# Reversing the score matmuls of the third query block in a fused state read and gated causal attention, with a new table of the order of steps

## The chip, the cores and the metric

The kernel runs on one core of one Trainium2 chip. The core has a matrix engine (TensorE, in the rows PE, with its weight loads as PEld), VectorE (DVE), ScalarE (ACT), GpSimd (POOL) and SyncE (SP). Each works through its own list of instructions in order, and semaphores make one engine wait for another. Here SP issues all DMA transfers, those that transpose among them. The metric is the device time of one execution in microseconds (us). The profiled execution of the kernel before took 310.0 us; its trace covers a span of 308.2 us of it.

## The reference

`x` is 8 batches x 8 heads x 512 rows x 64, `state` is 8 x 8 x 32 x 64. The reference has two stages:

```
a     = softmax(x @ state^T / 8);  xread = a  @ state     (512 rows read 32 slots)
a2    = softmax(state @ x^T / 8);  sread = a2 @ x         (32 slots read 512 rows)
y     = concat(xread, sread), heads side by side          (8, 544, 512)
logits = y @ w_gate;  w = softmax of the two largest of 4 (top 2 of 4 experts)
out   = sum over the two experts e of  w_e * (softmax(causal(q_e @ k_e^T / 8)) @ v_e) @ wo[e]
        with q_e = y @ wq[e], k_e = y @ wk[e], v_e = y @ wv[e], head width 64
```

`wq` and `wk` are drawn 200 times larger than the other weights, so the scores of the experts are large and need about fp32 accuracy.

## The kernel before, in words

Every fp32 operand of a large product is split into a high and a low f16 part, and a product is three f16 matmuls (high x high, high x low, low x high, `PROD`). The splits, the softmax and the evictions from PSUM are shared by ACT, DVE and POOL. Matrices that a product needs transposed (`xT`, `a2t`, `qm`, `pt`, `z`) are made by SP's transposing DMAs from their untransposed f16 form (`xh`, `a2`, `qh`, `ph`, `zh`).

A batch goes through these functions: `load` (its `xn` tiles of 512 KB and the state `sn`), `front` (scores against the state, their block transposes `eb` and maxima `mb` on DVE, the softmax `at`, the state's products with the weights `gs`, then `kt`, `qf` to `qh` to `qm`, and `v` as products of `at` and `gs`), `state_scores` and `side` (the slots that read the rows: `m`, `e`, `a2`, `a2t`), `probs` (causal scores of query blocks of 128 rows), `reads` (the probabilities times `v`, then times `wo`, then the store of `o`) and `tail` (the 32 state rows of two batches at once). `probs(b, unit)` is called for the units (0, 1), (2,) and (3,), which are the blocks of 128 query rows of a batch.

In `probs` (the lines around 811 to 866) the scores of the experts go to two PSUM banks `sp[0]` and `sp[1]`. A bank belongs to one of the two chosen experts of a row; three of the four experts can be that one, and the queries of those not chosen are zero. One step of PE does all of it: first matmuls that use all 128 rows of the array (two of the three experts at once), then the causal mask, added by a matmul with an identity, and then matmuls with 64 rows (the third expert), in pairs for the two banks that stand side by side in the upper and the lower half of the array. Then DVE takes the maxima (`mx`), ACT the exponentials (`p`), ACT and POOL or DVE split them into `ph`, and SP transposes `ph` to `pt` for `reads`.

The order of the work is not that of the code. The functions only record steps, 1959 in all. A step has an engine or a choice of engines (`either`: for example a multiplication of 192 columns on DVE or three of 64 columns on ACT). The function `run`, line 257, replays them by three packed tables in `ORDER`, line 22: the order of all steps, the engine that was chosen for each, and the buffer that each tile takes. All instructions are issued in `run`, so nearly every row of the trace has line 265 and tells its step only by its operand names. The buffer of a tile sets what it must wait for: the earlier readers of the same buffer, and with eight PSUM banks (`bank`) that is the most common wait of PE. On SP a transfer's issue also waits where the rings that it uses are still occupied.

Of the kernel before, what the change touches and what calls it, by code (L numbers as in the profile page):

```python
# [14 lines left out]
AF = mybir.ActivationFunctionType  # L15
# [8 lines left out]
        "c-jrtV`C5s6adico0pAc+peu;+qP|cwQSqAZQHhOzxVn4fs+CNQbKA#NCgDRfuR8iG=}=n6ch}afI~QF1eu^Agog-_9U?*`$PAGo2NZ-TkOy"
        "*OA;<zbAu9wxUWf|0Ar0ikT#ym+K_N;D>7g(bgM63=(?JkqgA5Q11)vC&fM!q*N<w}p3Z<Y7l!X@19O^;^$d45v8dQUh5FP4345$t<p$fEwS"
        "Wp^bLsh5;ai9~lf?f~;#i29Qgw{|V;zA{e2elwRw1L`?0NO$gNC;h^9rT4h&=tBtcSr>Npgr`59#8;#!zJhd1+g#=fSynY4?+<P!l7^(4nYV"
        "O#p5stu0Sv@fZb3Wk3ccJ276%#T!mvW7($^kT!)iz14`ggH~|A;EZl@$FdA;bZP){6pd=25J1`2y!7x||iD43qfPHWn?m`j>gQ+kX7Qrc)1|"
        "wk#9DwOi3Kzo+*a>4`CM<!|Fa*xSEU1d(VLue6voIS<V?mk&=U^4wgSk)!=fQm_i)&y$T!3o00v^ChSc<FRB2>q<uo0F*4J<<Ipd2oPO|Ti("
        "!%AF+6QCvrLV4T*MQJ%agjKi!CPENxh1IwmgQ)`6!WCE%>tiw62F<V>Rl?fX3b#XJObQKf4YtPS*aR!%T1*BZR0o@48;ry)a2+<p;#8iVL0z"
        "nZ>#-%)!_riN8es`)i%;M=l%yBX2{&MSd<oy69lnAt7@0fcBZ$JK=rxp~H_!ne!&~T%PvJYfgR;~Ie?Uj<iCwV=Zp8P%*bn>SPl&*uVH5s>F"  # L30
        "Yp_N;AZ>^192!0!frSgKfoUl{0qY{B3C5E!Pp-SC*p8){0JkkDviW&Sc$e^6B>Y@U>t^GO&W!OlW;Un$1vQAV{j@W#^M?@4QC?Z3=H6Z5SyD"
        ")be@ORXck7oxI7;h;B1V_ad<q&;{cq1+i?yyqv{k7BTG~akF_W{Zo}rZ5ToH-+<}WQKE~k5*ny^CbgWJBIR-|c1h^RMPzp?lEoccw#$Ff`>r"
        "zT=NfB@-cBIbKiDF@8szO~T6?Ub1v<rLV8mdo`DI!LsM7SG!&{}Fht!NK+qjj_wThmG0hYcwTwW0kOlMmo}YD5PyF-E~tm>M@wV~UN3@H9rH"
        "!x%tmFcL-Mo)nGFU`A|9NAN6mr|5JH+fi&vf^jGY#lhp)p5oF*ib*H17saB?coffJJlaJ4C=<q~OPGKYP!{Y@2`Ld}#XwApiRnBhp@f_b`%o"
        "Zd;sG>`Hd9hc#z`?5CFkChh?7%dPQimHicF^zl!Q}qc1%gbXa=RCK)!$vF%2c<%={WJV=7KfSvVO!!k*lhw$Meqg2Sm75236)m{N0Zev6MWj"
        "M8BrPD^p|4aSlun2!4LR+>o(WDJE;Y>6ugWdvQtI5LYy(L0PT@nj^8rh$}=XH!HOOX)F@q^F_OkH=9Ad5YONzKo~-oP%@V1WLp2aU!MVNtBU"
        "3U<Mk%Uoj^>!%UQuGt*?sLf0@IKgR%>N8j-}=HdmEmD2Nex-L;=DP^NvG=*Zy4U8sp=o{X|<usLk;9MHW+36O}rwp8fa?>`tjrn*PW#k>Sf("
        "mm%zJoX91?J{E@(~Mhe$K-SDX|pbm$-=TVqVTkc_@hQN)cX3*<>*l<;EP$PbG=mlU0;e0;L$Il%$eMmQYE~E={-@CzD5#Lw;gvxi68VDVOCm"
        "GKib=YRXGM$z=$);CuKBQ^;VxkEQv66z5!+Q~F35et;GEx;~atjI@)UNo9T_M13Wfgm6D$D#2Aax11!QN?e}HaeqlGN)>p3<dI#JS3Y4n*-b"
        "V0p`@2RRFkh#2H8uWF{7NKeYBr`<7ukJ2WTh{luUAvu5(p38YGA43{~U9bW^JHF>1}%C<C6Q+T50p&~v#Z=cp6c;p=ps>hcZ#gSU9F)Z^Q7o"  # L40
        "a*xpYQQ(CA$Q?M+>%@IUpzra=>oN5r(4v9GfP)4C^xx1XOW8(j&Ac6?!fuv4i}QUTto`XJ^F_)B)=4u+tiUea{&pG4>Cl8<-K&{KXQkP$yE)"
        "Jm-3Kq=y18O#pN~qmaF`j-bi=8OU-12yroC<Rvz$B`73wy3AL10a*5u_1N|rWskwZVhgw43&_lk)!{jM_rBZT_Kgnf!#4V(iyu#OVpL=j?xk"
        "6>+89mZ(R9c4dQ!TEK`L2GJcT`U9X$gI%U!<&jr+hS=-%|y7!k{C#ygaA;R7FN|Nv$L$r2tiyDg2bH$qx$Us`6Y>KhP*1&5t#VfgjLR{zzYC"
        "3|EwAOj<)q=~y1e-{d)$)^_rOr}1|ot}Y#<wjjS`))(}O7ujo`&NbyHz2PT1o@a1ZdCN1I`5o7hAM%Udb9ec`;i-()m5Ka`g+I|pp1^bYr__"
        "?qTu)~47ycz*`6Y>drr$K1Rp;>nt}mwF_zN}=<?lR)8_ExEBtN;V{^G{cL?-bc`pr$HjV$DH+E)IsYkTP?J!B1|7*FP#+EKRgEnUZdsgvB+M"
        "I25S+gk1{i+KmX&?UT`BWpzct<HaWDU)=Oml|F_Xe3?6<+Z0o(0?3`m-Bo5qX&4cebnXlMk{C~&7x8Dldj;mI-mdQXYD1~HJV1zgPc_Z^bqI"
        "K750x-*?Jx+uPBEe<}bR=Ug=7Er<FCQZZMDy94fu#wN})XJWBrQXbF?zwp3YG+Zg#mW2J<Nl(ccO#<Kk%H<g_nUB}BR-pH%DlueLp8e3y3+A"
        "f|b@wK$YQnFJVSHJ3RKEjh^nQmf}gc?Iv=uwWNiFCOp)-$}(Cd+g=&HtkXY7#ADXE}j>)0Dc0<LOHMuA6y=tkQElMP|x*{-KL>3m@ZknoMVj"
        "%X*zH$#trfwS2lkH`yFXrAc*~gp<XZLR0GknJcR`ji%MDoKBb6JSnV8ZM}t;qMBYa=rY^O8Fh{R)J(ci=1XSHrMY#j{?f&=QS)n%ZqmG3&Nk"
        "~J*`h_XfNs@rwoUi(b}gt&Bv>QcQaR31Exaw09a>0>X*63dYU?G6MX;T+LN<z7L<_JG-E1pmr@BS5!?MM8%PQGzC-?&IvJG;~qT3!jDp@Ro9"  # L50
        "FbkJNsh^CiD}1eudR{IvfZj^Ry$!kY^&|GJ+ehkS~lA&*=?&Fm#VtWs_7}KuF?D=@8^Az!(vzs&1vQB5}&qxR#R)~ev56jb(hAn_;$eR=owq"
        "0yS0h#(deGgVt8FmWc4(r@71^#$F|8qtFN)Vp*Gchn!p-qGd-Y*t-0>kv(`Xc=s`UzhpeR@(m*?Bhi$u@<h9aPV|xc(Cyn*I?3WXg#8O%uKP"
        "M;UuwIakdQn<wC%q(bJ(+dZc-C6`Xcs-A!!$hi)1%r~4@fFYYW=m1rnat{+)~&89ii=XxaP5edQ1;WK1*Zm^|*G^w01~FYC0=yp_<+<%L&b3"
        "MJ=OcvYwjDPHJX5CAqD;p3?l5*D6>g8>fS`vK6o*7GwqOik#L$7HskSh)vL9c3LjkC=IcMeoo{2QLAWIC6QmZ1m4we*m=8bXY{I#*9%s~y7@"
        "J`Xt(T&jn<nsQGeNOo1|5(hhOGuHd)U|b!%e3t%mi`^V&;mT5qjoXSKF9wK~?!>e?S`Zhx(wwXpiu((c#=ZEFqeqCT+h-pU%<6T4@v?Vr7{M"
        "+W}PX6P$>YK`o!y|nw**xJ}bdv34oy}hw^#{SmY+bsQHGgW<ue6)A=$@<u5o2_4Ln9b3z*4O&kH~Vf8{D=KCbn-|(SH&Z`d4C(Mk==cOMez<"
        "c(57fO5AY#+O-5KxA8ujV(R%qvi|YNnzjv|$9%|#Pvpu#hHp+VYJniG1ysM43Zr0PrXn3Eh-7T?CuxZ-ECR$&gWRq>65Ayk%#0UFy?PWte(0"
        "kiZ9qQ?Pfe!PeKFEf9G9Te1J=8~ea=)abJ-v^%FrQ&#JcVcQ%i7t;dPX1TsePel@{~T_2ir{R;;DRsXZBe((P!Hb%kFb5i)ZyImdhvkWY6YP"
# [9 lines left out]
        "c-l=<36_O02qUcbzwv~i-|2g5Tec*i!6U23?hCh=t~5Tdn(+!V7+=G0wS5Z?bF(zWn0J{mg)B{H=i302&ju?*?z<~z_*&c7!COuVVBr4T0AW"
        "bl1AAyj(JR|9yrD0W?mQZrho~*Mi87oHLF{*qD>i&3!X1YvBYD5odV$?qlb5#spzbYS{xNUcd{zX{x)%QMEV;5q@oGsRW5Ea6D4f+;mD|P5D"
        "BcnpOOt7s`|cnTL+nMseR0X$MHfgku1Gn;=LAfW6zA2S3IfHmQ?infMPiE%cvBPvn^3lviDbu*B#|>IDO}G}Q8f34vA)&g%O*VP9%pJw&ZF@"  # L70
        "-m!X}cMK?4^$C1@)LpwAn?aahhFk#@@c<MnE?FDblO?`GiX!uucn^?a&v$y;WqNIBU<QApn09a4zdKDT|2m17(RilVUTkCg<O>?xZS4V}e7T"
        "<QU@pX~p=#!ER5}Z@KJ(oGNq}_H*+V$Mzy2O(x#8k_YNA73mK!qTYYJUW~{{(+fQU*="
# [979 lines left out]
```

## Time and profile before

| what | value |
|---|---|
| runs of the kernel before | 305.06, 307.17, 308.19 us (median 307.17) |
| profiled execution | 310.0 us |
| its span in the trace | 308.2 us |
| PE busy | 285.8 us (93%), 3323 matmul records |
| DVE, ACT, POOL busy | 260.0 (84%), 226.1 (73%), 151.9 (49%) us |
| DMA packets | 165260, of them 144096 under 512 B; 53.95 MB |
| mean granted clock of PE | 0.983 |

A granted clock of 1.00 is the higher of TensorE's two levels, 2.4 GHz; the lower one is 1.2 GHz. A row of an engine gives the start in us, the duration, the engine and line, what is written and read (`out<-in`), the shape, and how many such instructions follow one another; in brackets stands the idle time before them, and the engine or transfer whose end released them.

### The profile page before, as it was taken

The page shows a single profiled execution, that of the slowest core. Times are in us where ns is not written, and L with a number is a line of the kernel's source. Part 1 is how long each engine was busy: PE and PEld are TensorE (multiplying, and loading weights), DVE is VectorE, ACT ScalarE, POOL GpSimd, SP SyncE. Part 2 cuts the span into 40 slices and gives each one's busy share as a digit, 9 for nine tenths or more (in the row PEclk, how much of TensorE's full clock was granted, in tenths as well). Part 3 has the DMA queues.
Part 4 walks back from the last instruction along what each step waited for, and adds up shares of the span by engine and source line. Part 5 has one row for each costly group of instructions (what it writes and reads, how often), then busy time and mean ns, then how long its engine had stood idle before and what let it go on. Part 6 is the DMA issues. An engine that isn't in the chain of part 4 may idle for free.

```text
span 308.2 us, 8993 instructions
## 1 busy us (share of the span) xinstructions
PE 285.8 (93%) x3323; PEld 193.7 (63%) x3323; DVE 260.0 (84%) x745; ACT 226.1 (73%) x690; POOL 151.9 (49%) x222
## 2 busy tenths in 40 slices
...
GB/s 194 223 124 203 154 156 183 234 177 172 138 202 203 168 180 213 171 177 197 207 142 245 185 234 175 125 185 178 83 146 176 91 209 126 95 172 205 184 213 152
DMA packets 165260, 53.95 MB, mean 175 GB/s; under 512 B 144096, under 2 KB 160736, under 8 KB 165216
## 3 DMA queue, kind: packets, MB, share of 16 engines
q1 hardware_dynamic: 165216, 53.37, 89.2%
...
q14 instruction: 18, 0.15, 0.2%
...
## 4 chain that ended last, share of the span: by engine, by line
PE 46%; DVE 21%; DMA 14%; ACT 12%; issue 4%; POOL 3%; SPq 0%; DVEq 0%; ACTq 0%; POOLq 0%
PE bank L265 46%; DMA xn<-in_x_dram 4%; DMA qm<-qh 4%; DVE mx L265 3%; DMA a2t<-a 3%; ACT p L265 2%; ACT z L265 2%; DMA pt<-ph 2%; DVE xh L265 2%; DVE mb L265 2%; DMA z<-zh 1%; DVE eb L265 1%; DVE qf L265 1%; DVE sbm L265 1%; DVE z L265 1%
## 5 line engine op out<-in xcount | busy, mean ns | idle before, releaser
L265 PE MATMUL bank<-kt,qm 128*128 128x128 f16 (+7 forms) x384 | 48.4, 305 | 4.6 <-DMA qm<-qh 4.0
L265 PE MATMUL bank<-gs,at 128*128 128x260 f16 (+3 forms) x368 | 50.7, 284 | 1.1 <-DVE eb L265 0.7
L265 PE MATMUL bank<-wo_n,z 128*128 128x512 f16 (+1 forms) x198 | 46.5, 373 | 2.8 <-DMA z<-zh 2.3
L265 PE MATMUL bank<-v,pt 128*128 128x192 f16 x480 | 45.5, 251 | 2.7 <-DVE kt L265 1.5
L265 PEld LDWEIGHTS <-pt 128*128 128x128 f16 x480 | 41.0, 100 | 6.7 <-issue 4.0
L265 PEld LDWEIGHTS <-at 128*128 128x128 f16 x336 | 32.1, 98 | 8.5 <-issue 2.3
L265 ACT ACTIVATE p<-bank,mx 128x128 f32<-128x128 f32 (+3 forms) x64 | 33.3, 526 | 4.3 <-DVE mx L265 3.9
L265 PEld LDWEIGHTS <-qm 128*128 128x128 f16 (+1 forms) x384 | 23.5, 98 | 18.7 <-DMA qm<-qh 4.6
L265 DVE TENSOR_REDUCE mx<-bank 128x1 f32<-128x128 f32 (+3 forms) x64 | 28.8, 478 | 7.7 <-PE bank L265 7.3
L265 POOL TENSOR_TENSOR ph<-p,ph 128x768 f16<-128x768 f32 (+1 forms) x15 | 28.1, 1875 | 7.4 <-ACT ph L265 4.8
L265 PEld LDWEIGHTS <-z 128*128 128x128 f16 x198 | 18.1, 98 | 21.7 <-DMA z<-zh 3.8
L265 ACT ACTIVATE o<-bank 128x512 f32<-128x512 f32 x30 | 17.8, 596 | 11.9 <-PE bank L265 11.8
L265 ACT ACTIVATE z<-bank,c 128x64 f32<-128x64 f32 x87 | 20.4, 320 | 6.8 <-PE bank L265 6.1
L265 ACT ACTIVATE xh<-xn 128x512 f16<-128x512 f32 x32 | 19.1, 629 | 7.3 <-DMA xn<-in_x_dram 6.4
L265 PE MATMUL bank<-at,gs 128*128 128x512 f16 (+1 forms) x92 | 24.2, 399 | 0.3 <-DVE m L265 0.3
L265 DVE SCALAR_TENSOR_TENSOR xh<-xn,xh 128x512 f16<-128x512 f32 x27 | 19.5, 741 | 3.9 <-ACT xh L265 3.8
L265 POOL TENSOR_TENSOR qh<-qf,qh 128x768 f16<-128x768 f32 x11 | 18.4, 1680 | 5.0 <-ACT qh L265 4.9
L265 POOL TENSOR_TENSOR eb<-eb,sbm 128x512 f32<-128x512 f32 x11 | 12.4, 1130 | 13.4 <-DVE sbm L265 12.0
L265 POOL TENSOR_TENSOR z<-z 128x128 f32<-128x128 f32 x15 | 7.0, 468 | 21.7 <-DVE z L265 9.5
L265 ACT ACTIVATE ph<-p 128x768 f16<-128x768 f32 (+1 forms) x17 | 15.6, 918 | 2.1 <-DMA pt<-ph 2.1
L265 ACT ACTIVATE gs<-bank 128x512 f16<-128x512 f32 (+2 forms) x29 | 13.7, 496 | 4.7 <-PE bank L265 4.6
L265 PEld LDWEIGHTS <-xh 128*128 128x128 f16 x416 | 15.1, 101 | 2.1 <-issue 0.8
...
## 6 DMA issues: line engine op xcount, KB each, us to landing
...
z<-zh SPq DMA_TRANSPOSE x29, 2.8
xT<-xh SPq DMA_TRANSPOSE x28, 3.3
...
```

The costliest lines, as they stand in the source:

```text
L265: f(**{k: v.ap() if isinstance(v, View) else v for k, v in kw.items()})
```

## The change

For the unit (2,) alone, the third block of every batch, the step of `probs` is issued in reverse: the pairs of 64-row matmuls first (now with the flag that starts the bank), then the masks, and the 128-row matmuls last (now with the flag that ends it). In the pairs of all units the upper half's matmul now stands ahead of the lower half's. The sizes passed to the planner's record follow. The three tables of `ORDER` are new: another order of steps, another engine for some, other buffers. The code below is the whole of the first part; of the tables one line stands for all.

```
@@ ORDER @@
-        "c-jrtV`C5s6adico0pAc+peu;+qP|cwQSqAZQHhOzxVn4fs+CNQbKA#NCgDRfuR8iG=}=n6ch}afI~Q...
+        "c-jrtgJKX06adico0pAc+peu;+qP|cwQSqAZQHhOzjwakqyT`FkQxwD0YP$LXaE9@L7_evGy#XE5DpqaCI...
...
@@ probs @@
+        turned = unit == (2,)
+        wide, paired = [], []
         for m, (a, c) in enumerate(PROD):
             for i in unit:
                 for s in range(2):
-                    g.append((part[s, i], qm[:, i, a, 2 - 2 * s], kt_[:, c, 1 - s, :w_[i]], m == 0 and i == i0, False))
-        for i in unit:
-            for s in range(2):
-                g.append((sp[s][:, at_[i] + i * P:at_[i] + w_[i]], identb, consts["maskb"], False, False))
-        for m, (a, c) in enumerate(PROD):
-            for i in unit:
-                g.append((part[1, i], qm[lo_, i, a, 1], kt_[lo_, c, 1, :w_[i]], False, m == 2))
-                g.append((part[0, i], qm[hi_, i, a, 1], kt_[hi_, c, 0, :w_[i]], False, m == 2))
-        st.mm(g, *((6, w_[i], 128, 1) for i in unit), (2 * nb, P, 128, 1), *((6, w_[i], 64, 2) for i in unit))
+                    wide.append((part[s, i], qm[:, i, a, 2 - 2 * s], kt_[:, c, 1 - s, :w_[i]], not turned and m == 0 and i == i0, turned and m == 2))
+                paired.append((part[0, i], qm[hi_, i, a, 1], kt_[hi_, c, 0, :w_[i]], turned and m == 0, not turned and m == 2))
+                paired.append((part[1, i], qm[lo_, i, a, 1], kt_[lo_, c, 1, :w_[i]], turned and m == 0, not turned and m == 2))
+        masks = [(sp[s][:, at_[i] + i * P:at_[i] + w_[i]], identb, consts["maskb"], False, False) for i in unit for s in range(2)]
+        full = [*((6, w_[i], 128, 1) for i in unit), (2 * nb, P, 128, 1)]
+        half = [(6, w_[i], 64, 2) for i in unit]
+        if turned:
+            st.mm(paired + masks + wide, *half, *full[::-1])
+        else:
+            st.mm(wide + masks + paired, *full, *half)
```

The number of matmuls stays at 3251, and the steps that they belong to keep nearly the same order on PE: 264 of its 305 steps stand where they stood, the others move by a few places. On the other queues more moves, and 187 of the 1959 steps change their engine; DVE issues 716 instead of 742 steps, ACT 521 instead of 518, POOL 232 instead of 209. Changes between the array's shapes along PE's list (128 rows, 64 rows, 32 rows, fewer columns) are 115 before and 117 now.

Three places of the new order. The first is DVE's list where the state scores of batch 4 are transposed (`eb_115` from two banks, the second of them bank_85), while the maxima `m` and `mb` of the same scores are taken and the last `kt` of batch 3 leaves its bank (`kt_135`). Before:

```order
L265 TENSOR_REDUCE m_0_145<-bank_85 128x1
L265 STREAM_TRANSPOSE eb_115<-bank_82 128x256
L265 TENSOR_SCALAR m_0_145<-m_0_145 128x1 [waits DVE_49]
L265 STREAM_TRANSPOSE eb_115<-bank_85 128x256
L265 STREAM_TRANSPOSE eb_115<-bank_85 128x256 [waits Activation_49]
L265 TENSOR_REDUCE mb_116<-eb_115 128x16 [waits DVE_49]
L265 TENSOR_REDUCE m_0_145<-bank_82 128x1
L265 TENSOR_REDUCE mb_116<-eb_115 128x16 [waits DVE_49]
L265 SCALAR_TENSOR_TENSOR kt_135<-bank_83,kt_135 128x512 [waits Activation_49]
```

The same piece of DVE's list in the changed kernel:

```order
L266 TENSOR_REDUCE m_0_145<-bank_85 128x1
L266 SCALAR_TENSOR_TENSOR gs_121<-bank_86,gs_121 128x260 [waits Activation_49]
L266 SCALAR_TENSOR_TENSOR gs_121<-bank_79,gs_121 128x260 [waits Activation_49]
L266 TENSOR_REDUCE mb_116<-eb_115 128x16 [waits DVE_49]
L266 STREAM_TRANSPOSE eb_115<-bank_85 128x256 x2
L266 SCALAR_TENSOR_TENSOR kt_135<-bank_82,kt_135 128x512 [waits Activation_49]
L266 TENSOR_REDUCE m_0_145<-bank_83 128x1
L266 TENSOR_REDUCE mb_116<-eb_115 128x16 [waits DVE_49]
L266 SCALAR_TENSOR_TENSOR kt_135<-bank_80,kt_135 128x512 [waits Activation_49]
```

The two transposes of bank_85 now follow each other without a wait for ACT between them, and `kt_135` stands ahead of one `m` and one `mb` that it stood behind.

The second place is SP's list while batch 2 is read and batch 3's queries are transposed: `pt_0_168` and `pt_0_169` are probabilities of batch 2 (units (2,) and (3,)), `qm_134` from `qh_142` and `qh_143` the two halves of batch 3's queries, `xn_89` a load of batch 6. Before:

```order
L265 DMA_TRANSPOSE pt_0_155<-ph_153 128x12x128 [waits DMAHW3_49,DVE_49]
L265 DMA_TRANSPOSE pt_0_168<-ph_154 128x12x128 [waits DMAHW4_49,Pool_49]
L265 DMA out_dram<-o_181 128x512 [waits DMAHW5_49,Activation_49]
L265 DMA_TRANSPOSE qm_134<-qh_142 128x12x128 [waits DMAHW6_49,Pool_49]
L265 DMA sn_87<-in_state_dram 128x2x64 [waits DMAHW7_49]
L265 DMA xn_89<-in_x_dram 128x8x128 [waits DMAHW0_49]
L265 DMA_TRANSPOSE pt_0_169<-ph_153 128x16x128 [waits DMAHW1_49,Pool_49]
L265 DMA_TRANSPOSE xT_96<-xh_92 128x8x128 [waits DVE_49,DMAHW2_49,PE_49,Activation_49]
L265 DMA out_dram<-o_179 128x512 [waits DMAHW3_49]
L265 DMA_TRANSPOSE qm_134<-qh_143 128x12x128 [waits DMAHW4_49,Pool_49]
```

The same piece of SP's list in the changed kernel:

```order
L266 DMA_TRANSPOSE pt_0_155<-ph_153 128x12x128 [waits DMAHW2_49,DVE_49]
L266 DMA_TRANSPOSE xT_96<-xh_95 128x8x128 [waits DMAHW3_49]
L266 DMA out_dram<-o_181 128x512 [waits DMAHW4_49,Activation_49]
L266 DMA xn_89<-in_x_dram 128x8x128 [waits DMAHW5_49]
L266 DMA_TRANSPOSE qm_134<-qh_142 128x12x128 [waits DMAHW6_49,Pool_49]
L266 DMA_TRANSPOSE pt_0_168<-ph_154 128x12x128 [waits DMAHW7_49]
L266 DMA sn_87<-in_state_dram 128x2x64 [waits DMAHW0_49]
L266 DMA_TRANSPOSE pt_0_169<-ph_153 128x16x128 [waits DMAHW1_49,Pool_49]
L266 DMA_TRANSPOSE xT_96<-xh_92 128x8x128 [waits DMAHW2_49,DVE_49,Activation_49]
L266 DMA_TRANSPOSE qm_134<-qh_143 128x12x128 [waits DMAHW3_49,Pool_49]
```

The transpose of `pt_0_168` moves from ahead of the first `qm_134` to behind it and behind the load `xn_89`; the second `qm_134` no longer has a store of `o` ahead of it.

The third place is SP's list some 25 us earlier, where `qm_133` from `qh_142` and `qh_143` are batch 2's queries, `sn_87` a load of the state, `xT_96` from `xh_94` a transpose for batch 5 and `pt_0_169` probabilities of batch 1. Before:

```order
L265 DMA_TRANSPOSE pt_0_169<-ph_154 128x16x128 [waits DMAHW4_49,Pool_49]
L265 DMA_TRANSPOSE xT_96<-xh_94 128x8x128 [waits DMAHW0_49,DVE_49,DMAHW5_49,PE_49,Activation_49]
L265 DMA_TRANSPOSE qm_133<-qh_142 128x12x128 [waits DMAHW6_49,Pool_49]
L265 DMA sn_87<-in_state_dram 128x2x64 [waits DMAHW7_49]
L265 DMA_TRANSPOSE qm_133<-qh_143 128x12x128 [waits Pool_49]
```

The same piece of SP's list in the changed kernel:

```order
L266 DMA_TRANSPOSE pt_0_169<-ph_154 128x16x128 [waits DMAHW4_49,Pool_49]
L266 DMA sn_87<-in_state_dram 128x2x64 [waits DMAHW5_49]
L266 DMA_TRANSPOSE xT_96<-xh_94 128x8x128 [waits DMAHW0_49,DMAHW6_49,DVE_49,PE_49]
L266 DMA_TRANSPOSE qm_133<-qh_142 128x12x128 [waits DMAHW7_49,Pool_49]
L266 DMA_TRANSPOSE qm_133<-qh_143 128x12x128 [waits Pool_49]
```

The load `sn_87` moves from behind the first `qm_133` to two places ahead of it.

Elsewhere on SP the transpose to batch 2's fourth `z` moves ahead of one `pt` and one `a2t`. On PE the last product of `side` (`a2t,xh`, 48 matmuls, batch 7) moves ahead of the product of batch 4's fourth `z` with `wo`. On ACT, two of the conversions `xh<-xn` of batch 5 move ahead of the high half of the `kt_135` above, and the exponential `e` behind it. At the start ACT's high half of batch 0's last `kt` moves two places ahead, and on PE one more product moves ahead of its reader.

## Rows read from the trace of the kernel before

**Rows 1.** The page: busy time and share of each engine, and the DMA packets.

```profile
PE 285.8 (93%) x3323; PEld 193.7 (63%) x3323; DVE 260.0 (84%) x745; ACT 226.1 (73%) x690; POOL 151.9 (49%) x222
...
DMA packets 165260, 53.95 MB, mean 175 GB/s; under 512 B 144096, under 2 KB 160736, under 8 KB 165216
```

**Rows 2.** Chain that ended last: start, length, and what the time went to.

```profile
64.10 6.71 DMA qm<-qh
...
150.91 4.40 DMA qm<-qh
...
171.15 4.34 DMA z<-zh
...
245.91 59.10 PE bank L265 x565
```

**Rows 3.** Stretches: length, busy time (count) of PE, PEld, DVE, ACT, POOL, clock, DMA share, GB/s.

```profile
71.20:74.80 3.60, 3.60 (x51) 2.27 (x48) 1.27 (x6) 1.20 (x5) 1.72 (x5) 0.53 0.88 184
112.00:119.00 7.00, 4.73 (x32) 2.96 (x31) 4.30 (x11) 4.36 (x13) 3.73 (x4) 1.00 1.36 179
119.00:122.60 3.60, 3.60 (x25) 3.37 (x24) 3.60 (x10) 2.02 (x7) 1.65 (x4) 0.53 0.98 212
123.00:130.00 7.00, 7.00 (x62) 4.01 (x62) 5.10 (x16) 4.47 (x18) 3.83 (x6) 1.00 0.80 170
```

**Rows 4.** Timeline of PE: ends of a unit (2,) step, batches 2 and 4.

```profile
126.16 0.66 PE L265 MATMUL bank<-kt,qm 64*128 64x384 f16 x6
126.75 1.47 PE L265 MATMUL bank<-wo_n,z 128*128 128x512 f16 x6
...
194.31 0.66 PE L265 MATMUL bank<-kt,qm 64*128 64x384 f16 x6
194.81 0.28 PE L265 MATMUL bank<-tl,rep 64*128 64x4 f32 x2
```

**Rows 5.** Timeline of PE, 116 to 123 us.

```profile
116.40 0.82 PE L265 MATMUL bank<-gs,at 128*128 128x260 f16 x6 [0.74 <-DVE eb L265]
118.76 3.72 PE L265 MATMUL bank<-v,pt 128*128 128x192 f16 x24 [1.53 <-DVE kt L265]
```

**Rows 6.** Timeline of DVE, the same time.

```profile
115.90 0.45 DVE L265 STREAM_TRANSPOSE eb<-bank 128x256 f32<-128x256 f32 x1 [2.70 <-ACT e L265]
...
118.02 0.68 DVE L265 SCALAR_TENSOR_TENSOR kt<-bank,kt 128x512 f16<-128x512 f32 x1
```

**Rows 7.** Timeline of ACT, the same time.

```profile
114.57 0.63 ACT L265 ACTIVATE xh<-xn 128x512 f16<-128x512 f32 x1 [2.78 <-DMA xn<-in_x_dram]
```

**Rows 8.** Timeline of SP: start and length of an issue.

```profile
116.14 1.34 SPq L265 DMA_TRANSPOSE qm<-qh  x1
117.53 1.08 SPq L265 DMA_DIRECT2D sn<-in_state_dram  x1
...
140.55 1.47 SPq L265 DMA_TRANSPOSE qm<-qh  x1
...
144.33 4.44 SPq L265 DMA_TRANSPOSE pt<-ph  x1
...
150.23 0.58 SPq L265 DMA_DIRECT2D out_dram<-o  x1
```

**Rows 9.** Timeline of PE: other places at which it waits, and one read of `pt`.

```profile
36.29 0.38 PE L265 MATMUL bank<-kt,less 128*128 128x512 f16 x1 [2.16 <-ACT kt L265]
...
147.97 1.65 PE L265 MATMUL bank<-v,pt 128*128 128x192 f16 x18
...
155.36 1.15 PE L265 MATMUL bank<-kt,qm 128*128 128x384 f16 x6 [1.41 <-DMA qm<-qh]
...
175.53 1.47 PE L265 MATMUL bank<-wo_n,z 128*128 128x512 f16 x6 [1.65 <-DMA z<-zh]
...
222.14 0.97 PE L265 MATMUL bank<-kt,qm 128*128 128x384 f16 x5 [0.61 <-DVE v L265]
...
240.97 1.47 PE L265 MATMUL bank<-wo_n,z 128*128 128x512 f16 x6 [0.62 <-DMA z<-zh]
```

More of the change, by code (lines that the diff above doesn't have):

```diff
@@ L23 @@
     (
[L24 to L58, printed above, removed]
@@ L67 @@
-    (
[L68 to L72, printed above, removed]
+        "c-jrtgJKX06adico0pAc+peu;+qP|cwQSqAZQHhOzjwakqyT`FkQxwD0YP$LXaE9@L7_evGy#XE5DpqaCI}A=Ap&HF%n%WBKtad?ksuEgf}D"
@@ new lines @@
+        "^WvqD}-19>qU<br&d5AtAINDqaf0_4X+lpE4P4afkIAtRK70#FQ!LNh1>MIb+vg(wgLbszv*Kyhde6`>SVg%S`IT0%4^3DF@4szXPp3B8~dl"
+        "!o$92|7Uxs0T5j7PN+7hy|UY8pMV;&<EN;TxbjNpbNx@cF-5PLN}-j-Jw17gWAv^5<nH`0R^x(T!Icz5DVh~=m~}JAQZt<5QIbF5L|}iP!xk"
+        "P1VdprT!BGw60SmVEQVv@2wa1`umeWH0=N!Gp#<K5W3UTG!wI+v!(bc?hn;W>2EuJf2xnj_B!WE<1_fy$l*Bu*4+g_Dm;__sE-Zq>kQk=JWL"
+        "OL%-~g1uDKH*J!Vs7NOW-t|hqEvfO5-djO#7iK7NOZt2IoL!SOxcBE}Vn1I1kpqeOL-BU_MmC3$PL%z*1Zd7oj??g^f@S*TFJO0-IqItcR6Y"
+        "1B=o!2%;@80m|b;sENyA1FXV{uoYHg1q`O;SP@rXecT4cs2MiKK&XY=p%qrb=2#ocQ3H&`Nue?}!DJ9Zt#J)D#THlx*J2wiPV2BCmZxV>7pv"
@@ new lines @@
+        "fUEKT*W0=2{v)D|1zb0|rXxf5={C-4YfKzn=%-=GUVhF4IEqVQ`dL!I#rJcaJ~7QRC}EKBd81NOlm&=EIcPkawuk+CoSgdVsFBk(Wiho9j$Y"
+        "{r531%}{P_y9w35dML&7?FozHx&E}iWO-v_D93vI1xWWRdTFE<FFcyz%AH>CgDi@1T|>@hT<p;hocd2I))+Q7>vbJu?9`UnMfGG|6m5j=BBh"
+        "A=V4r)h0%FD&c_8<ouYCa4#3$MkK<u@Y({f1vMj{O7zrm}E!v9Fumd%x_&680;Ue6D$+0#?#l@Ha<8vK~!4YT*M#s7o11nPtT7n6&7pBCR*q"
+        "K_=PV7h#Fa<`WDij$zQ7o)SU1$v@!miYc>eE_Eg^_6&uA_+9fOcbR>WzD_8|}p&)P_!CL)wS?F*Qb^^%Rp2U?WP50dx>gVPo1rvGEX|#;DYt"
+        "4r3aOMA7INM!{%&1~Xz?icUxHEXJVN)RWp#9EyWUusy}4jTDoPV=szDneiN+z@r$CHc>yygz@P-Ucv;NfU;mhN<@7q5ED~>%8HvQ2_@ugn28"
@@ new lines @@
+        "f{AWfrWoD`!-Qc6b2IWecj<dlL3(EyrGDJTi2<digwGIJ`*j)6RbF5p8<%4z5|X5mzv3@_tg>P>xV2wlM~)RR+FTzrICxfiGA-h2_?U|M>M!"
+        "zmp;#xUx`v1AOr!vr#uo?u^&Epa6sZKV+uN>?$V%%V6lipJ7NiYL)!Hf7_X6j4S~ddklIIFSsb^f-=UNDh9A?{PfEm+jP_({K*VKojU0W~8q"
+        ";kv?Ef9>6&<EoY)@n2s}37P^k}C>KA+tdyPuWC3NP?>LFR;Zlk!lj#QLqU$n+ZsIoDLCYzoOr<##P3F=q%uWM21Lvk6IG=9g3d+biC?7AQLH"
+        "q*mU_s8!`T2$v;*YqHUSeVy%z1bb72v}B6Yoei$w_xHF9&fEzAG!~7v`a?a$g#A5?M@7C72^gQGO)%B)c@@Kv_jiIHe5XRFYJdP*X0(%{iIm"
+        "kdk~4Q%iCw%PFJ<r;*hJlvDCjA9*09xj2{N`&fn_U`2i=*A=O+?4-w%3(Ip_=_e&PmxOR7CVC?Mr81wS+%lAzDzH!$9w6m-7b)eD-Si35NnY"
```

39 lines of the change are left out of this document (34 added, 5 removed).

## The prediction

> **What bounds the kernel now.** I read the page first [rows 1]: PE is busy 285.8 of 308.2 us, DVE 260.0. The reader sees that PE leads, but that its idle time, some 22 us, is made by others. The chain of waits [rows 2] says where: from 245.91 us to the end it is one piece of 59.10 us of PE, without a wait, so nothing after 246 us can be gained unless PE gets less to do. Before it the chain leaves PE at several places, most often for a transposing DMA that took 4.34 to 6.71 us. The table of stretches [rows 3] gives the second loss: from 71.2 to 74.8 and from 119.0 to 122.6 us the granted clock is 0.53, close to the lower level of 1.2 GHz, and before the second of them PE was busy only 4.73 of 7.00 us. 3.60 us at 0.53 cost 3.60 x 0.47 = 1.7 us against full clock. Last I read PE's own timeline at the waits [rows 5, 9] and the queues behind them [rows 6 to 8].
>
> **The reversed step.** The matmuls stay the same in number and size, so only the changes of array shape can count. A unit (2,) step of batch 2 ends with six 64x384 matmuls that take 0.59 us (126.16 to 126.75) where a 128-row one follows, and that of batch 4 takes 0.50 us (194.31 to 194.81) where a 64-row one follows [rows 4]: a change of shape costs 0.09 us. The step has one inner change either way round; the change at its start takes the place of the one at its end. The lists hold 115 changes before and 117 now, so +2 x 0.09 = **+0.2 us**. Batch 2's step now directly follows 64-row matmuls and saves changes, others lose as many and two more; the count holds both. Whether maxima can start earlier I cost at nothing: all readers wait for the step's last matmuls in both.
>
> What remains is the new table, taken wait by wait. The price of an altered wait has its lower bound at 0 (another wait takes its place) and its upper at the wait in the row.
>
> **The wait at 118.76.** This is the largest. DVE's second `eb` transpose stood idle for 2.70 us for ACT's `e` [rows 6], which stood behind an `xh` that waited 2.78 us for the load of `xn` until 114.57 [rows 7]; `kt` came on DVE only at 118.02, and PE waited 0.74 and 1.53 us [rows 5]. In the new order the transposes no longer wait between them and `kt` stands ahead of one `m` and one `mb`. On ACT two `xh` of that load now stand ahead of the high half of `kt`. With 0.63 for each [rows 7], as much again for the high half, all as upper values, `kt`'s high half ends at 114.57 + 3 x 0.54 = 116.2 (0.54 is my estimate of the step from start to start, a little under the row's 0.63), DVE adds 0.68 [rows 6], and `v,pt` starts at 116.9 in place of 118.76: 1.9 us. The idle time of PE falls from 2.27 to well under 1 us, so the clock need not fall, and the 24 matmuls would take 3.72 x 0.53 = 2.0 us in place of 3.72 [rows 5, 3]. Together 3.6 us.
> It is not all kept: a wait takes its place. About 0.8 us behind the `v,pt` (one six-matmul group like the 0.82 of [rows 5]) PE starts batch 2's scores, which need `qm`. Before, that is at 122.5 + 0.8 = 123.3. The issue of `qm` at 116.14 now has the `sn` load ahead of it, 1.08 us [rows 8] (the third place shown with the change), so it goes at 117.2 and lands 4.40 us later [rows 2], at 121.6. PE would be there at 118.9 + 0.8 = 119.7 and waits. So the gain at this place is 123.3 - 121.6 = **-1.7 us**, with bounds of -3.6 (no wait) and +0.6 (landing after 6.71 us [rows 2], at 123.9). I take -1.7, because 4.40 is the row for the same kind of transpose on the same queue.
>
> **The smaller ones.** At 155.36 PE waited 1.41 us for `qm` [rows 9], issued at 150.91 [rows 2]; the store of `o` ahead of it at 150.23 [rows 8] has gone, so -0.7 (bounds 0 and -1.41). At 175.53 it waited 1.65 us for `z` [rows 9], which now goes out ahead of a `pt` and an `a2t`; the product with that `a2t` is next on PE and comes later by as much, so I take -0.4 (0 and -1.65). At 222.14 it waited 0.61 for a bank that `v` had to leave [rows 9]; the step has another bank now, with readers that are done earlier: -0.6 (0 and -0.61). At 240.97 it waited 0.62 for `z` [rows 9]; the 48 matmuls of the next `a2t,xh` are moved ahead of this product, which covers it: -0.6 (0 and -0.62). At 36.29, PE waited 2.16 us for ACT's `kt`; that now stands two places earlier on ACT, but PE has the last query product ahead of it, whose bank DVE frees late. I see no clear sign and take 0 (bounds -1 and +0.5). The tail behind 245.91 has no wait to lose: 0.
>
> **What hides what.** The parts add to -1.7 - 0.7 - 0.4 - 0.6 - 0.6 = -4.0 us. Whatever PE gains it must not outrun: behind 123 us DVE is busy 5.10 of 7.00 us [rows 3], so there is slack of about a quarter, and over the span DVE is busy 84% [rows 1]. Next waits will take part of it back. I keep half, a choice between the bounds of nothing and everything: -2.0 + 0.2 = **-1.8 us** against the profiled 310.0, so 308.2. That execution lies 2.8 us above the median 307.17 of the three runs, so the forecast against the median is **305.4 us**. The case's own range is from 307.4 (nothing kept) to 303.4 (all kept).
>
> **Rivals.**
> *All is kept, and more (300 to 303.4, say 302).* The clock stays up at 119 us and at a second place such as 71.2 us [rows 3], and `qm` lands soon enough. Then -3.6 - 2.3 - 1.7 for one more stretch, +0.2, is -7.4 at the outside, 299.8; the middle between that and 303.4 is 301.6, say 302. For it: the list of DVE is shorter by 26 steps, and DVE's work is what frees the banks. Against: ACT and POOL take those steps, and `qm` behind `xn` at 64.10 is unchanged.
> *Nothing is kept, since transfers set the pace (307.4).* In the stretch of 112 to 119 us the 16 DMA engines have a share of 1.36 at only 179 GB/s [rows 3], and SP needs 4.44 us to issue one `pt` [rows 8]: transposes queue behind transposes. The packets stay, 144096 of 165260 under 512 B [rows 1]. If that sets when `qm` and `pt` land, then an earlier issue lands no earlier. Against: outside such stretches the share is 0.80 [rows 3], and PE is fully busy there. The change not doing what it says for the shapes (115 against 117) is in this case too.
> The Trainium skill, page "DMA: Bandwidth & Descriptors", section Specifications, asks for transfers of at least 512 B for the line rate. By that rule the many short packets would make this rival, and with it 307.4, the likelier one; the stretch with a share of 1.36 at 179 GB/s agrees with it, the one with 0.80 at 170 GB/s less so.
> *A new wait for `pt` (310.5, slower).* The place is SP's list around 140 us. The transpose of `pt` for batch 2's unit (2,) stood ahead of the first `qm`; now it stands behind that `qm`, issued at 140.55 for 1.47 us [rows 8], and behind the `xn` load. It goes out at 142.0 and lands at 146.4 with the 4.40 of [rows 2], but at 148.7 with the 6.71 of a transpose behind a load. PE reads it at 147.97 in the kernel before [rows 9], and 1 to 2 us earlier if the gain at 118.76 is kept. With 148.7 PE waits, loses 0.7 against before and, after up to 3 us of idling, the clock too, 1.7. If the same delay hits the `qm` above (+0.6), with the 0.2 it is +3.2: 310.4, about 310.5. It decides whether transposes behind a load land within 6 us here. For it: the row of 6.71 is just such a pair. Against: with 4.40 nothing happens.
>
> **Chances.** Forecast 0.38, all kept 0.27, nothing kept 0.15, the new wait 0.20. Differences under 1% (3.1 us) can't be told from no change. Below 304.1 lie nearly all of the second case (0.25) and a quarter of the first (0.09): faster 0.34. Above 310.2 lie over half of the last (0.12), and I leave 0.05 for a wait of that kind elsewhere in the new table: slower 0.17. The rest, 0.49, is within 1%. The range takes in the case of more kept down to 301.0 and the new wait up to 311.0; what lies outside is about 0.2.
>
> **What would show it.** In the changed profile the DVE wait of 2.70 us for `e` should be gone, `v,pt` x24 should start near 117 and take about 2 us at a clock of 1.00 in that stretch, and a wait for `qm` should stand behind it. The waits at 175 and 241 us for `z` should be smaller or named `a2t`. Six 64-row matmuls ahead of the masks should take as long as before. PE's tail should still be some 59 us without a wait. The forecast is wrong if the granted clock still drops near 119 us or at a new place, if a `pt` wait stands near 148 us, or if the tail begins later than 245.91.

## The result, and the profile after

The changed kernel took 304.99 us (median of 13 runs, 302.82 to 306.72), the kernel before in the same runs 308.19 us (13 runs, 305.06 to 309.79). The ratio is 0.9906, with a 95% interval of 0.9877 to 0.9936: about 2.9 us less by the ratio. The profiled execution of the changed kernel has a span of 301.9 us and a mean granted clock of 0.999. That of the kernel before (310.0 us, 0.983) counts as a slow run, which the length of its stretches at the lower clock fits.

The page of the changed kernel, busy times and packets:

```profile
PE 282.6 (94%) x3323; PEld 189.0 (63%) x3323; DVE 252.6 (84%) x719; ACT 226.4 (75%) x699; POOL 163.4 (54%) x244
...
DMA packets 165259, 53.94 MB, mean 179 GB/s; under 512 B 144096, under 2 KB 160736, under 8 KB 165216
```

Against [rows 1] DVE has 7.4 us less and POOL 11.5 us more; the matmuls are the same and the packets but for one. The stretches of the changed kernel (length, busy time and count of PE, PEld, DVE, ACT, POOL, granted clock, DMA share, GB/s):

```profile
71.00:75.00 4.00, 4.00 (x64) 2.64 (x62) 3.17 (x9) 3.40 (x12) 2.89 (x4) 1.00 1.00 124
112.00:119.00 7.00, 5.14 (x47) 3.96 (x46) 6.91 (x16) 5.44 (x17) 2.60 (x4) 1.00 1.07 211
119.00:123.00 4.00, 4.00 (x49) 3.01 (x48) 3.92 (x9) 3.07 (x13) 1.72 (x3) 1.00 0.92 217
123.00:240.00 117.00, 114.67 (x1386) 78.17 (x1385) 104.52 (x313) 97.50 (x311) 78.23 (x103) 1.00 0.92 175
```

The two stretches at 0.53 of [rows 3] are gone. The profiled execution of the kernel before had a third one, behind the wait of 2.16 us at 36.29 [rows 9], which is gone as well:

```profile
37.00:41.00 4.00, 4.00 (x62) 3.31 (x68) 4.00 (x11) 3.72 (x15) 3.75 (x4) 0.57 0.75 189
```

PE's timeline near 117 us, the answer to [rows 5]:

```profile
113.80 1.71 PE L266 MATMUL bank<-gs,at 128*128 128x260 f16 x12 [1.05 <-DVE gs L266]
116.27 0.82 PE L266 MATMUL bank<-gs,at 128*128 128x260 f16 x6 [0.77 <-ACT e L266]
116.94 2.14 PE L266 MATMUL bank<-v,pt 128*128 128x192 f16 x24
118.92 0.83 PE L266 MATMUL bank<-gs,at 128*128 128x260 f16 x6
119.58 1.15 PE L266 MATMUL bank<-kt,qm 128*128 128x128 f16 x12
```

DVE and ACT at the same place, the answers to [rows 6, 7], first DVE:

```profile
114.59 0.76 DVE L266 STREAM_TRANSPOSE eb<-bank 128x256 f32<-128x256 f32 x2
115.28 0.65 DVE L266 SCALAR_TENSOR_TENSOR kt<-bank,kt 128x512 f16<-128x512 f32 x1
```

ACT:

```profile
112.40 1.15 ACT L266 ACTIVATE xh<-xn 128x512 f16<-128x512 f32 x2 [2.29 <-DMA xn<-in_x_dram]
...
113.55 0.58 ACT L266 ACTIVATE kt<-bank 128x512 f16<-128x512 f32 x1
...
115.44 0.69 ACT L266 ACTIVATE e<-bank,m 128x512 f32<-128x512 f32 x1 [1.02 <-DVE eb L266]
```

The wait of 2.70 us on DVE has gone, now `e` waits for `eb`; the 24 `v,pt` matmuls start at 116.94 and take 2.0 us (116.94 to 118.92). No wait for `qm` follows. SP's issues there and around 140 us, the answer to [rows 8]:

```profile
112.53 0.63 SPq L266 DMA_DIRECT2D sn<-in_state_dram  x1
...
114.68 3.41 SPq L266 DMA_TRANSPOSE qm<-qh  x2
...
139.47 1.57 SPq L266 DMA_TRANSPOSE pt<-ph  x1
...
142.54 2.06 SPq L266 DMA_TRANSPOSE pt<-ph  x1
...
146.38 1.50 SPq L266 DMA_TRANSPOSE qm<-qh  x1
```

PE at other places, with the longer of its waits, the answer to [rows 9]:

```profile
39.06 1.56 PE L266 MATMUL bank<-a2t,xh 128*128 128x64 f16 x48 [1.54 <-DMA a2t<-a]
...
69.81 1.16 PE L266 MATMUL bank<-kt,qm 128*128 128x128 f16 x12 [1.86 <-DMA qm<-qh]
...
144.40 1.66 PE L266 MATMUL bank<-v,pt 128*128 128x192 f16 x18 [0.17 <-DMA pt<-ph]
...
150.56 0.74 PE L266 MATMUL bank<-kt,qm 64*128 64x384 f16 x6
...
172.55 1.56 PE L266 MATMUL bank<-a2t,xh 128*128 128x64 f16 x48 [1.51 <-DMA a2t<-a]
...
236.31 1.46 PE L266 MATMUL bank<-wo_n,z 128*128 128x512 f16 x6
```

Behind 123 us the waits for `qm` (1.41), `z` (1.65 and 0.62) and for `v`'s bank (0.61) are gone. One wait for `a2t` stands in place of that for `z`; the `pt` that the last rival feared costs 0.17 us. Ahead of 123 us nothing is saved: the waits that PE's timeline marks with a releaser add there to 12.4 us before and to 12.6 us in the changed kernel, at other places.

### The profile page after: what moved, and what is told of

The parts are those of the page before. It is cut to its first block, busy times and chain, and to the rows that moved or that the text cites. A ratio compares the mean times of both kernels' runs of the same rounds, so it can differ in the third digit from the quotient of the medians.

```text
span 301.9 us, 9002 instructions
## 1 busy us (share of the span) xinstructions
PE 282.6 (94%) x3323; PEld 189.0 (63%) x3323; DVE 252.6 (84%) x719; ACT 226.4 (75%) x699; POOL 163.4 (54%) x244
## 2 busy tenths in 40 slices
DMA packets 165259, 53.94 MB, mean 179 GB/s; under 512 B 144096, under 2 KB 160736, under 8 KB 165216
## 5 line engine op out<-in xcount | busy, mean ns | idle before, releaser
L266 PE MATMUL bank<-v,pt 128*128 128x192 f16 x480 | 44.3, 246 | 1.3 <-DMA pt<-ph 0.8
L266 PEld LDWEIGHTS <-pt 128*128 128x128 f16 x480 | 39.6, 98 | 5.9 <-issue 2.5
L266 POOL TENSOR_TENSOR ph<-p,ph 128x768 f16<-128x768 f32 (+1 forms) x17 | 31.2, 1839 | 9.7 <-ACT ph L266 4.7
L266 ACT ACTIVATE z<-bank,c 128x64 f32<-128x64 f32 x96 | 22.9, 324 | 4.8 <-PE bank L266 2.4
L266 DVE SCALAR_TENSOR_TENSOR xh<-xn,xh 128x512 f16<-128x512 f32 x28 | 21.4, 774 | 5.1 <-ACT xh L266 5.1
L266 POOL TENSOR_TENSOR z<-z 128x128 f32<-128x128 f32 x22 | 10.8, 489 | 23.9 <-DVE z L266 18.0
L266 ACT ACTIVATE o<-bank 128x512 f32<-128x512 f32 (+1 forms) x31 | 18.0, 585 | 7.2 <-PE bank L266 7.1
L266 POOL TENSOR_TENSOR zh<-z,zh 128x256 f16<-128x256 f32 x22 | 16.1, 736 | 4.7 <-ACT zh L266 4.1
L266 PEld LDWEIGHTS <-xh 128*128 128x128 f16 x416 | 13.9, 98 | 7.3 <-issue 2.6
L266 ACT ACTIVATE ph<-p 128x768 f16<-128x768 f32 (+1 forms) x20 | 18.2, 910 | 0.2
L266 POOL TENSOR_TENSOR eb<-eb,sbm 128x512 f32<-128x512 f32 x11 | 11.5, 1046 | 10.1 <-DVE sbm L266 9.4
```

What stands on the lines that cost most here:

```text
L266: f(**{k: v.ap() if isinstance(v, View) else v for k, v in kw.items()})
```

## The experiments

All of them are compared with runs of the kernel before on the same chip (the two tables cut at 123 us on one, those cut at 193 us on another). "Kernel before" and "changed kernel" stand for their code or their `ORDER` tables, as named.

**The code and the table apart.** The first kernel has the changed `probs` with the tables of before, the second the other way round:

```
  e1_turn_only                         e2_table_only
  probs: changed                       probs: before
- ORDER: changed                     - ORDER: before
+ ORDER: before                      + ORDER: changed
```

> The reversed unit (2,) step with the tables of the kernel before (same order, engines and buffers). Theory A (the time comes from the table): the reversed step alone moves the time by less than 0.5 us; with 0.09 us a change of shape and batch 2's saving, batch 4's loss, between -0.2 and +0.4 us, ratio 0.998 to 1.002. Rival B (the reversal frees PE or starts the softmax earlier): at least half of the 3 us, ratio 0.995 or less.

> The code of the kernel before with the new tables. Theory A: as fast as the changed kernel, ratio 0.987 to 0.994. Rival B (the reversal carries the gain): ratio 0.997 or more.

Measured: the reversed step alone 307.99 us, ratio 1.0026 (0.9992 to 1.0060); the table alone 304.39 us, ratio 0.9897 (0.9849 to 0.9945). The whole gain is the table's. What the change is named for does nothing that can be measured; 1.0026 is a little above the expected 1.002, within the noise.

The first of the two has the order of the kernel before and ran at full clock (a mean of 1.000), so it is also a second profile of that order. Its stretches:

```profile
71.00:75.00 4.00, 4.00 (x63) 2.72 (x62) 3.28 (x11) 2.77 (x10) 2.67 (x3) 1.00 1.07 114
112.00:119.00 7.00, 5.47 (x53) 4.37 (x52) 6.26 (x15) 6.89 (x24) 3.52 (x5) 1.00 1.07 215
119.00:123.00 4.00, 4.00 (x41) 2.39 (x39) 3.45 (x10) 2.19 (x9) 2.19 (x4) 1.00 1.22 209
123.00:246.00 123.00, 115.11 (x1408) 79.22 (x1406) 111.69 (x333) 97.94 (x311) 71.96 (x90) 1.00 0.89 169
```

The stretches at the lower clock at 71 and 119 us of [rows 3] are not there in every execution of this order: here PE waits 2.90 us for `qm` near 70 us and 1.53 us for `kt`, and the clock stays at 1.00. And a large part of this order's loss sits elsewhere: from 123 to 246 us PE is idle 123.00 - 115.11 = 7.9 us, in the changed kernel's 123 to 240 us only 117.00 - 114.67 = 2.3 us.

**The place near 118 us, by itself.** In the kernel before, two moves in the table; in the changed kernel, the same backwards:

```
  e3_eb_in_before (before's code and table)   e4_eb_out_of_after (changed code and table)
  ACT: e  moved behind kt's high half         ACT: e  moved ahead of kt's high half
       and behind both eb transposes               and between the two eb transposes
  DVE: kt moved ahead of m and mb             DVE: kt moved behind m and mb
```

> The kernel before with one place altered: ACT's first exponential e of batch 4 behind the high half of kt and behind both eb transposes, DVE's kt ahead of one m and one mb. Theory A (this place is the largest part): v,pt x24 starts near 117 in place of 118.8 us, the clock stays at 1.00 there, and 1 to 3 us are kept to the end, ratio 0.990 to 0.997. Rival (transfers set the pace): the place moves but the end by less than 0.5 us, ratio 0.998 to 1.002, with a wait for qm or pt behind it.

> The changed kernel with that one place put back to the order before: e between the two eb transposes and ahead of kt, DVE's kt behind m and mb. Theory A: the wait ahead of v,pt x24 returns with some 2 us and 1 to 3 us of the gain are lost, ratio to before 0.994 to 1.000. Rival: the time stays at the changed kernel's, 0.987 to 0.993.

Measured: mended in the kernel before 307.82 us, ratio 1.0017 (0.9982 to 1.0052); broken in the changed kernel 304.41 us, ratio 0.9889 (0.9852 to 0.9925). Both are as if nothing had been done, so theory A falls. The timelines of PE show where it went. First the order of before at full clock (`e1_turn_only`):

```profile
113.24 0.82 PE L264 MATMUL bank<-gs,at 128*128 128x260 f16 x6
115.59 2.14 PE L264 MATMUL bank<-v,pt 128*128 128x192 f16 x24 [1.53 <-DVE kt L264]
...
121.73 1.46 PE L264 MATMUL bank<-wo_n,z 128*128 128x512 f16 x6
```

The same with the place mended (`e3_eb_in_before`):

```profile
113.81 0.82 PE L264 MATMUL bank<-gs,at 128*128 128x260 f16 x6 [0.58 <-ACT e L264]
114.47 2.14 PE L264 MATMUL bank<-v,pt 128*128 128x192 f16 x24
...
120.12 1.15 PE L264 MATMUL bank<-kt,qm 128*128 128x384 f16 x6 [0.80 <-DMA qm<-qh]
...
121.91 1.47 PE L264 MATMUL bank<-wo_n,z 128*128 128x512 f16 x6
```

The wait for `kt` is gone and `v,pt` starts 1.1 us earlier, as expected; 5 us on, PE waits 0.80 us for the second half of `qm`, which it did not before. The product `wo_n,z` that follows this step starts at 121.73 in the one and at 121.91 in the other (the step itself is turned in `e1_turn_only`, so its own rows don't compare): the lead is gone. In the changed kernel with the place broken, the waits return (0.92 us for `eb`, 0.94 for `kt`), and the wait for `a2t` near 173 us shrinks from 1.51 to 0.50, its matmuls starting at 172.38 against 172.55: the lost time was slack for a transfer later on.

**Which part of the table.** A mixed table takes the steps of one order up to a cut and the rest in the other order, with the engines and buffers of each:

```
  h1_old_then_new:  ORDER = before's steps up to 123 us + the new table's rest
  h2_new_then_old:  ORDER = the new table's steps up to 123 us + before's rest
```

> The changed code with a mixed table: the order, engines and buffers of the kernel before for the steps up to about 123 us, those of the changed kernel behind. In two executions at full clock PE waited, in stretches that its timeline marks with a releaser, 9.7 us before and 11.3 us with the new table ahead of 123 us, and 7.8 against 1.9 us from there to 246 us. Theory C (the gain sits behind 123 us, the first part gains nothing): ratio 0.981 to 0.991, as fast as the changed kernel or up to 2 us faster. Rival A (the part up to 123 us with the eb place carries at least half): 0.994 or more.

> The other mixture: the new table up to about 123 us, the one before behind. Theory C: no gain, 0.998 to 1.006, with the waits for qm near 151 and for z near 166 and 172 us back. Rival A: 0.996 or less.

Measured: old then new 303.52 us, ratio 0.9886 (0.9844 to 0.9928); new then old 308.59 us, ratio 1.0045 (1.0008 to 1.0082). Theory C holds: the part up to 123 us gains nothing, by itself it may even lose a little. PE's five longest waits of the two kernels behind 123 us, first old then new, that is the new part of the table:

```profile
128.88 1.47 PE L264 MATMUL bank<-wo_n,z 128*128 128x512 f16 x6 [0.90 <-DMA z<-zh]
144.69 1.65 PE L264 MATMUL bank<-v,pt 128*128 128x192 f16 x18 [0.15 <-DVE gt L264]
151.05 0.66 PE L264 MATMUL bank<-kt,qm 64*128 64x384 f16 x6 [0.23 <-DVE mx L264]
172.11 1.56 PE L264 MATMUL bank<-a2t,xh 128*128 128x64 f16 x48 [0.64 <-DMA a2t<-a]
208.91 1.16 PE L264 MATMUL bank<-kt,qm 128*128 128x128 f16 x12 [0.22 <-DMA qm<-qh]
```

New then old, that is the old part:

```profile
133.81 0.81 PE L264 MATMUL bank<-gs,at 128*128 128x256 f16 x6 [1.03 <-DVE bd L264]
153.69 0.66 PE L264 MATMUL bank<-kt,qm 64*128 64x384 f16 x6 [1.59 <-DMA qm<-qh]
167.70 1.47 PE L264 MATMUL bank<-wo_n,z 128*128 128x512 f16 x6 [0.55 <-DMA z<-zh]
174.67 1.47 PE L264 MATMUL bank<-wo_n,z 128*128 128x512 f16 x6 [2.15 <-ACT ph L264]
207.61 1.65 PE L264 MATMUL bank<-v,pt 128*128 128x192 f16 x18 [0.95 <-DVE gs L264]
```

The first five add to 2.1 us, the second five to 6.3 us (7.7 with the shorter ones). The waits go with the part of the table behind the cut, whatever stands ahead of it.

Could the gain be the clock? The new order keeps it up more often: of the 69 executions of the kernel before beside the kernels of this section 20 have a mean granted clock of 0.998 or more and 42 have 0.993 or 0.994, as the profiles with one stretch at the lower level have; of the 18 of `e2_table_only` and `e4_eb_out_of_after` 16 have 0.998 or more. But among the executions at 0.998 or more on the chip of these two, the kernel before still takes 306.9 us in the mean (7 of them) and they take 304.3 (16), so 2.6 us remain. And old then new gains with 0.993 or 0.994 in five of its six executions, while new then old gains nothing with 0.998 or more in nine of twelve. The clock is not the main part.

The new part was cut once more, at 193 us:

```
  h3_new_from_193:     ORDER = before's steps up to 193 us + the new table's rest
  h4_new_123_to_193:   ORDER = before's + the new table's between 123 and 193 us + before's
```

> Changed code, table of the kernel before up to about 193 us, the new one behind. By the waits of PE in an execution at full clock (0.95, 0.50, 0.43 and 0.54 us there before, 0.3 after) the gain of this part is at most 2.1 us: ratio 0.992 to 0.999. If the parts add up, this run's gain and that of the next one sum to the 3.5 us of the mixed table.

> Changed code, the new table only for the steps between about 123 and 193 us, the one before on both sides. PE waited there 0.94, 1.23, 1.63 and 1.53 us, and with the new table 0.90, 0.15, 0.23 and 0.64: a gain of 3.4 us if these add, ratio 0.986 to 0.993. If the waits behind grow instead: 0.996 or more.

Measured: from 193 us on 305.27 us, ratio 0.9935 (0.9898 to 0.9973); between 123 and 193 us 305.67 us, ratio 0.9951 (0.9912 to 0.9991). The parts add: 0.65% and 0.49% make 1.14%, as the mixed table's 1.14%; with intervals of 0.4% either way and another chip for the mixed table, that they meet so closely is chance. In the later part the gain is that of the sum of the waits (2.0 us against at most 2.1). In the earlier part it is 1.5 us where the waits promised 3.4, a miss of the expected ratio; its interval reaches to 2.7 us. Where the rest of those 3.4 us went stays open. The waits were read from one execution of `e1_turn_only`, which took 307.95 us; the 20 executions of the kernel before at 0.998 or more took 306.5 in the median, so it may have waited more than most, which isn't shown.

Open too is what in the new table removes these waits: its order of steps, its choice of engines (DVE has 7.4 us less to do) and its buffers were cut only together.

The profile of `h3_new_from_193` has the lower clock near 118 us that `e1_turn_only` with the same order up to there has not. Its PE timeline:

```profile
114.40 0.82 PE L264 MATMUL bank<-gs,at 128*128 128x260 f16 x6 [0.71 <-DVE eb L264]
116.76 3.59 PE L264 MATMUL bank<-v,pt 128*128 128x192 f16 x24 [1.53 <-DVE kt L264]
```

Here a wait of 0.71 us stands ahead of the 1.53, as the 0.74 in [rows 5], and the same 24 matmuls take 3.59 instead of 2.14 us; in `e1_turn_only` only the 1.53 us stand there.

**Two transfers moved in the changed kernel.** One line of SP's list each:

```
  e5_a2t_first                          e6_qm_first
+ a2t_149<-a_0_150                    + qm_134<-qh_142
  pt_0_168<-ph_153                      xn_89<-in_x_dram
- a2t_149<-a_0_150                    - qm_134<-qh_142
```

> The changed kernel with one transfer moved: the transpose a2t of batch 5 goes out ahead of the pt that stood before it (about 1.5 us earlier). In the changed kernel PE waits 1.3 to 1.5 us for it near 173 us. If the order of SP's list sets these waits: that wait falls below 0.5 us and the time falls by 0 to 1.2 us, ratio to before 0.983 to 0.991. If the transfers' pace sets it (it lands no earlier): the wait stays above 1.0 us, ratio as the changed kernel's, 0.988 to 0.993.

> The changed kernel with the transpose qm of batch 1 (first half) moved ahead of the 512 KB load xn that stood before it. In the changed kernel PE waits 1.7 to 1.9 us for it near 70 us. If a transpose behind a load is late (6.7 us in the prediction, against 4.4): the wait falls by 1.0 us or more. What is gained at 70 us should be given back by 123 us if theory C holds (the stretch up to there is not set by PE's waits one by one): ratio 0.987 to 0.993; otherwise 0.983 to 0.988.

Measured: `a2t` first 303.93 us, ratio 0.9886 (0.9838 to 0.9935); the wait for `a2t` near 173 us is gone from the timeline. The transpose lands 4.9 us after its issue, against 5.0 in the changed kernel, and issued earlier it lands earlier: the order of SP's list sets this wait, not the pace of the transfers. On the time it can't be told from the changed kernel. `qm` first 304.12 us, ratio 0.9881 (0.9827 to 0.9934), again as the changed kernel. Its PE timeline near 70 us:

```profile
67.52 1.16 PE L264 MATMUL bank<-kt,qm 128*128 128x128 f16 x12 [0.75 <-DMA qm<-qh]
...
73.39 0.67 PE L264 MATMUL bank<-kt,qm 64*128 64x384 f16 x6 [1.98 <-DMA qm<-qh]
```

The wait of 1.86 us falls to 0.75, and one of 1.98 us for the second half of `qm` appears. Directly behind the load the first half landed 5.6 us after its issue, ahead of it 4.5; the second half, behind the load in both, took 3.8 us before the move and 5.5 after it. The wait has moved from one transpose to its neighbour.

**A better version.** The mixed table of `h1_old_then_new` with the place near 118 us mended and `a2t` first:

```
  b1_mixed_best:  h1_old_then_new + ACT: e behind kt, DVE: kt ahead of m and mb + SP: a2t ahead of pt
```

> The mixed table (old up to 123 us, new behind) with two more edits: the eb place mended (e behind kt, kt ahead of m and mb) and the a2t transpose of batch 5 ahead of pt. If the eb place gives its gain back to the qm behind it as in the earlier run, and the a2t wait of 0.64 us is all there is left: 0 to 0.7 us below the mixed table, ratio 0.983 to 0.990. If the gains add freely: 0.975 to 0.982.

Measured: 302.21 us, ratio 0.9852 (0.9805 to 0.9899), within the first expectation. It is the lowest ratio of all, but its interval overlaps those of the mixed table and of the changed kernel, so that it beats the changed kernel isn't shown; that it beats the kernel before is.

**The price of a change of shape.** In the kernel before, every score step is altered so that it alternates between 128-row and 64-row matmuls:

```
  for m, (a, c) in enumerate(PROD):
      ... the 128-row matmuls of product m
+     if m == 2: the masks
+     the 64-row pairs of product m
- the masks
- for m ...: the 64-row pairs of product m
```

> The kernel before with its table, but in every score step (24 of them) the 128-row and the 64-row matmuls alternate product by product: 211 changes of shape in place of 115, same matmuls. At 0.09 us a change PE has 96 x 0.09 = 8.6 us more to do; part of it falls into PE's waits (some 17 us ahead of 246 us): 4 to 9 us slower, ratio 1.013 to 1.030. If the 0.09 us was not the change of shape: within 1 us, ratio 0.997 to 1.003.

Measured: 313.56 us, ratio 1.0213 (1.0156 to 1.0270), 6.4 us slower, within the expectation. Its page, PE:

```profile
PE 290.7 (94%) x3323; PEld 186.4 (60%) x3323; DVE 262.4 (85%) x745; ACT 226.6 (73%) x690; POOL 151.3 (49%) x222
```

The same line of the order of before at full clock (`e1_turn_only`):

```profile
PE 282.0 (92%) x3323; PEld 189.3 (62%) x3323; DVE 259.8 (85%) x745; ACT 226.0 (74%) x690; POOL 152.0 (50%) x222
```

290.7 - 282.0 = 8.7 us for 96 changes is 0.09 us each, and some 2 of the 8.7 us fell into waits that PE had anyway.

## Why the prediction was right, and where it was not

**The forecast and the range.** 305.4 us was forecast, 304.99 measured; the fall of 0.9% lies inside 1%, the likeliest class. The forecast's own difference was -1.8 us, the measured one about -2.9. That the totals meet within 0.4 us is partly luck: the forecast starts from a median of 307.17 us of three runs, and the kernel before had 308.19 in the 13 runs beside the changed one.

**The reversed step** was priced at +0.2 us. Right: by itself it does nothing measurable (1.0026, interval across 1), and 0.09 us a change of shape, read from two rows [rows 4], was found again with 96 changes.

**The wait at 118.76** was the largest term, -1.7 us. The local part came out nearly to the digit: `v,pt` at 116.94 against 116.9, the 24 matmuls in 2.0 us, the wait of 2.70 us gone. The wait for `qm` that should follow did not come: it was issued at 114.68, not at 117.2, and landed in time. As a term of the sum the place was wrong: mended alone it gives nothing, broken alone it costs nothing. Two steps failed. The first is the price of the clock: -1.7 us of the 3.6 came from a stretch at 0.53 that stands in the profiled execution [rows 3] and in one more of the six profiles with this place as it was, not in the other four. The difference worked out with this stretch was then carried to the median, 2.8 us below the profiled execution, although that one had three stretches at the lower clock (the third, at 37 us, the prediction did not see) and most others lose what one costs. The second is what was kept. "A wait takes its place" was said, but for the first half of `qm`, and only in part; `e3_eb_in_before` showed it for the second half, and all of it given back by 122 us.

**The smaller ones** were summed to -2.3 us for the places at 155, 175, 222 and 241 us. They carry the gain: the table behind 123 us alone gives 3.5 us. Their waits went as described: `qm` at 155 and `z` at 241 without a wait, `z` at 175 replaced by `a2t`, with a remainder of 1.51 us. For the `qm` at 155 more than the store of `o` had gone: the `pt` ahead of it held SP's list for 2.06 us in place of 4.44, and it went out 4.5 us earlier. The sum was too small: in the full-clock profile of the old order there are waits behind 123 us that it left out (0.94 us near 131, 1.63 us near 166, 0.95 us near 205; the last stands in the profile that it was made from too, 0.94 us at 208.16), and in the changed kernel they are gone as well.

**"I keep half"** gave a good total by two errors against each other, which is luck: half of a term of 1.7 us that is worth nothing, and half of terms of 2.3 us that are worth 3.5. The runs put in its place: nothing is kept ahead of 123 us, nearly everything behind 193 us, about half between.

**The rivals.** "Nothing is kept, since transfers set the pace" holds up to 123 us in its result; whether by its reason stays open. Near 70 us moving `qm` only handed the wait on to its neighbour, which fits it; at 173 us moving `a2t` shows that an earlier issue does land earlier, so there the pace of the transfers is not the reason. The packets under 512 B are as many as before, 144096, and the time fell. The new wait for `pt` was there with 0.17 us: the transpose went out at 139.47, not at 142.0, and landed 4.9 us later, where it was feared only if such a transpose took over 6 us. "All is kept" did not come, and a part of it, the clock near 119 and 71 us, comes and goes with the execution.

**The other signs.** The six 64-row matmuls ahead of the masks take 0.59 to 0.60 us to the next row, as those before that a 128-row one follows, in six of the seven batches in which they stand alone in the timeline (0.67 at 150.56). From 240 us to PE's last matmul, which ends at 298.7, one wait of 0.24 us stands; the tail has no wait to lose, as said.
